# GpSimd makes the remainders of the first half of expert 2's weights

## The chip, the cores and the metric

The kernel runs on one core of a Trainium2 chip. The metric is the device time of one execution in microseconds (us). Three timed runs of the kernel before gave 667.23, 667.99 and 668.74 us, median 667.99 us. One further execution was profiled; it took 665.24 us, and its span, from the first to the last instruction, is 663.5 us.

## The reference

Three stages on 1536 tokens of 512 numbers, all in float32:

```
a   = softmax(mask(q k^T / 8 + bias)) v          # 2 x 8 heads, 768 positions, 96 local + 8 global
x   = (silu(x w_gate) * (x w_val)) w_out         # d_ff = 1536
e   = argmax(x w_router);  g = softmax(...)[e]   # 8 experts, one for each token
out[mask_e] = g * sigmoid(x w_output_gate)[e] * (relu(x[mask_e] w1[e]) w2[e])
```

`w1[e]` is 512 x 1024 and `w2[e]` is 1024 x 512. The last stage, the experts, is where the change lies.

## The kernel before

**Numbers in two parts.** TensorE multiplies in the format fp32r. So that no digits are lost, every operand is kept as a rounded part and a remainder: `whi` is the weight rounded to fp32r (ScalarE, line 637), and `wlo = raw - whi` is what rounding left (VectorE, line 640). A product is then summed from `whi*xhi`, `wlo*xhi` and `whi*xlo`.

**Weights of an expert.** They come in four transfers of 1 MB (`m2_raw`, line 643): g = 0 and 1 are the halves of `w1[e]`, g = 2 and 3 those of `w2[e]`. Each fills one `raw` buffer, and there are three of those in rotation, so the transfer after next can only be issued, on SP's queue, when both the rounding and the subtraction of an earlier buffer are done. Every buffer is made into two units of 128 x 1024 (`m2_units`), so an expert has eight units: eight roundings and eight subtractions. From unit 24 on (expert 3) a unit is cut into two pieces of 128 x 512. The first 24 units, of experts 0, 1 and 2, are whole.

**Work of an expert.** The tokens have been scattered to a table `xs` in memory by expert. For expert e, `m2_gather(e)` reads its 224 rows back (`xr`, 449.8 KB, line 957 through 538, issued by GpSimd); `m2_tokens(e)` copies each token's factor and index out of it (`fac` and `idt`, lines 963 and 964, VectorE), transposes the rows and splits them into two parts. `m2_up(e)` is the up product (line 995): its sums lie in four banks used in turn, `s0` and `s1`, then the two of `gv`; for each, ScalarE copies one half out and VectorE adds the other (`hs`, line 997), and only then may TensorE write that bank again. `m2_down(e)` is the down product (lines 1012 to 1014). Results `ot` are scattered to the output by GpSimd. Expert 0 goes another way, in two blocks of 128 tokens: `block_up` and `block_down` (lines 677 to 706), with `hh` and `hl` as the two parts of its hidden numbers and `ot` from line 705.

**What sets the order.** The code is written in the order gather of expert e+2, weights of e+1, and so on, but a scheduler of the language places each instruction in its engine's queue by its own reckoning, unless it is pinned. Every engine then works strictly in the order of its queue: an instruction that waits holds up all behind it. DMAs issued by GpSimd stand in GpSimd's queue among its arithmetic.

Of the kernel before, what the change touches and what calls it, by code (L numbers as in the profile page):

```python
# [15 lines left out]
ALU = mybir.AluOpType  # L16
# [17 lines left out]
def attn_moe_moe_kernel(  # L34
# [16 lines left out]
    nc = tc.nc  # L51
# [32 lines left out]
    def f(ap):  # L84
        return ap.bitcast(F32)
# [32 lines left out]
    def load_raw(src, dt, eng=nc.sync, after=False):  # L118
        rawn[0] += 1
        pool = rawb_p if wb_open and rawn[0] % 3 == 0 else raw_p  # L120
        raw = pool.tile([P, 2048], dt, tag="raw", name="raw")
        a = src.shape[0] // P
        ins = eng.dma_start(out=raw.rearrange("p (a c) -> p a c", a=a), in_=src.rearrange("(a p) c -> p a c", p=P))
        if after:
            tc.keep_in_program_order(ins)
        return raw
# [305 lines left out]
    def wv(ap, a):  # L432
        return ap.rearrange("p (a c) -> p a c", a=a)
# [187 lines left out]
    NWC = 4  # L621
    cnt = {"u": 0}

    def m2_unit(raw, after):
        n = cnt["u"]
        cnt["u"] += 1
        m = n
        n %= NWA + NWB + NWC
        pool = wb_p if n < NWB else wa_p if n < NWA + NWB else wc_p
        hi = pool.tile([P, 1024], F32R, tag="whi", name="whi")  # L630
        lo = pool.tile([P, 1024], F32R, tag="wlo", name="wlo")
        a = raw.shape[1]
        hv, lv = wv(hi, a), wv(lo, a)
        cuts = 1 if m < 24 else 2
        for x in range(cuts):
            o = slice(x * a // cuts, (x + 1) * a // cuts)
            ins = nc.scalar.copy(hv[:, o], raw[:, o])  # L637
            if after:
                tc.keep_in_program_order(ins)
            nc.vector.tensor_tensor(out=lv[:, o], in0=raw[:, o], in1=f(hv[:, o]), op=ALU.subtract)  # L640
        return hv, lv

    def m2_raw(e, g, **kw):
        src = w1[e][:, g * 512:(g + 1) * 512] if g < 2 else w2[e][(g - 2) * 512:(g - 1) * 512, :]
        return wv(load_raw(src, F32, **kw), 4)

    def m2_units(raw, g, after=False):
        return [m2_unit(raw[:, :, z * 256:(z + 1) * 256] if g < 2 else raw[:, 2 * z:2 * z + 2, :], after)
                for z in range(2)]

    def m2_weights(e, u=(), **kw):
        u = list(u)
        for g in range(len(u) // 2, 4):
            u += m2_units(m2_raw(e, g, **kw), g)
        return u[0:4], u[4:8]

    def scatter(src, idx):
# [162 lines left out]
    def m1_stream():  # L820
        for n in range(len(work) + 1):
            if n == len(work) - W0:
                w0.append(m2_weights(0))
# [107 lines left out]
    for _ in stream:  # L931
        pass
    u10, u20 = w0[0]
    ulast = m2_units(w0[1][0], 0, True)
    block_up(shl0, u10, hh0, hl0, scratch0, 2)
    tc.keep_in_program_order(nc.vector.tensor_copy(fac0, xr0[:, DM:DM + 1]))
# [120 lines left out]

    block_up(shl, u10, hh, hl, scratch)
    ulast += m2_units(w0[1][1], 1)
    xx1 = m2_tokens(1, nx)  # L1060
    late = [m2_raw(1, g, eng=nc.gpsimd, after=True) for g in (2, 3)]
# [6 lines left out]
    for e in range(1, NE):  # L1068
        (fac, xx), (u1, u2) = cur
        hh, hl = m2_up(e, xx, u1)  # L1070
        if e + 1 < NE:
            tk = m2_tokens(e + 1, nx)
            if e + 2 < NE:
                nx = m2_gather(e + 2)
            cur = (tk, m2_weights(e + 1))
        if e == 1:
            check_cover()
        m2_down(e, fac, hh, hl, u2)
# [306 lines left out]
```

## Time and profile before

| what | before |
|---|---|
| median of three timed runs | 667.99 us |
| the profiled execution | 665.24 us |
| its span | 663.5 us |
| TensorE busy (PE) | 632.7 us, 95% |
| VectorE busy (DVE) | 437.1 us, 66% |
| ScalarE busy (ACT) | 325.9 us, 49% |
| GpSimd busy (POOL) | 132.6 us, 20% |

Times in the rows below are microseconds from the start of the span. Expert 0's second block, and the start of expert 1, lie between 475 and 514 us; from 514 us on one expert follows another every 22 us.

### The profile page before, as it was taken

To read this page: it belongs to the slowest core of one execution; us is meant where nothing else is said; L and a number is where in the kernel's file an instruction comes from. 1 tells how busy PE (TensorE), PEld (TensorE's weight loads), DVE (VectorE), ACT (ScalarE), POOL (GpSimd) and SP (SyncE) were. 2 spreads that over 40 slices of the span, in tenths; PEclk is the share of its full clock that TensorE was granted. 3 is DMA by queue.
4 is the path that set the end of the run, shared out by engine and by line. 5 is a ranking of instruction groups with operands and counts; after the bars stand their busy time and mean duration, and the time that the engine had idled before them with its cause. 6 is when DMAs were issued, how large, how long until landed. Compare 5 with 4: busy or idle time off the path is not lost.

```text
span 663.5 us, 11770 instructions
## 1 busy us (share of the span) xinstructions
PE 632.7 (95%) x4433; PEld 547.1 (82%) x4433; DVE 437.1 (66%) x1087; ACT 325.9 (49%) x755; POOL 132.6 (20%) x180
## 2 busy tenths in 40 slices
PE   9899999999999999999999999998988999999993
PEld 8677678888888798999999999987866888888882
DVE  6899985666677998464364445555679777876330
ACT  4676866666665553131132222233467666766230
POOL 3414644444432420000000111001401100110011
PEclk9999999999999999999999999999999999999998
DMA  8779872210015545030010111122598767663000
GB/s 217 171 206 249 201 185 53 65 37 21 22 26 191 185 135 188 1 127 1 1 65 1 63 64 64 49 72 89 206 294 306 231 239 246 223 216 95 12 27 29
DMA packets 71587, 80.84 MB, mean 122 GB/s; under 512 B 43376, under 2 KB 43376, under 8 KB 71520
## 3 DMA queue, kind: packets, MB, share of 16 engines
q1 hardware_dynamic: 64960, 57.35, 30.3%
q0 software_dynamic: 6560, 22.64, 9.9%
q8 instruction: 37, 0.61, 0.4%
q14 instruction: 30, 0.25, 0.1%
HBM read 66.31 MB, written 14.26 MB: 121 GB/s over the span
## 4 chain that ended last, share of the span: by engine, by line
PE 40%; issue 34%; DVE 11%; DMA 8%; ACT 3%; POOL 2%; POOLq 0%; SPq 0%; DVEq 0%; ACTq 0%
PE ps_gv L446 6%; PE ps_gv L995 5%; DMA xs<-ypay,rw 3%; PE ps_av L396 3%; PE ps_s L995 3%; PE ps_y L995 2%; PE ps_tr L365 2%; PE ps_s L1013 2%; PE ps_s L1014 2%; PE ps_s L1012 2%; PE ps_s L334 2%; PE ps_y L1014 2%; PE ps_y L1012 2%; PE ps_y L1013 2%; DMA raw<-in_moe_w_dram 2%
## 5 line engine op out<-in xcount | busy, mean ns | idle before, releaser
L446 PE MATMUL ps_gv<-xlo,whi 128*128 128x256 f32 x576 | 164.2, 285 | 0.9 <-DVE xlo L403 0.9
L446 PE MATMUL ps_gv<-xhi,whi 128*128 128x256 f32 x576 | 164.6, 287 | 0.4 <-DVE hh L454 0.3
L446 PE MATMUL ps_gv<-xhi,wlo 128*128 128x256 f32 x576 | 164.5, 286 | 0.0
L446 PEld LDWEIGHTS ps_gv<-xlo,whi 128*128 128x128 f32 x576 | 109.8, 191 | 4.7 <-DVE xlo L403 1.3
L446 PEld LDWEIGHTS ps_gv<-xhi,whi 128*128 128x128 f32 x576 | 109.6, 191 | 4.6 <-DVE hh L454 0.5
L446 PEld LDWEIGHTS ps_gv<-xhi,wlo 128*128 128x128 f32 x576 | 110.1, 191 | 1.5 <-issue 0.3
L640 DVE TENSOR_TENSOR wlo<-raw,whi 128x512 fp32r<-128x512 f32 (+1 forms) x104 | 81.4, 810 | 18.5 <-ACT whi L637 16.5
L637 ACT CAST whi<-raw 128x512 fp32r<-128x512 f32 (+1 forms) x104 | 71.0, 721 | 34.5 <-PE ps_s L1014 11.6
L453 DVE SCALAR_TENSOR_TENSOR hh<-th,ps_gv 128x256 f32<-128x256 f32 x72 | 30.1, 418 | 74.9 <-ACT th L451 74.9
L451 ACT ACTIVATE th<-ps_gv 128x256 f32<-128x256 f32 x72 | 27.6, 384 | 88.1 <-PE ps_gv L446 87.9
L380 POOL TENSOR_TENSOR sp<-sp,rs 128x512 f32<-128x512 f32 (+1 forms) x48 | 47.8, 995 | 84.3 <-DVE rs L379 71.7
L457 ACT CAST hi<-hh 128x256 fp32r<-128x256 f32 x72 | 29.2, 405 | 56.6 <-DVE hh L454 52.7
L350 ACT ACTIVATE sp<-sp,mn 128x256 f32<-128x256 f32 (+1 forms) x96 | 46.6, 487 | 18.4 <-DVE mn L346 12.0
L611 POOL DMA_INDIRECT xs<-ypay,rw x12 | 11.9, 988 | 207.2 <-DVE rw L177 192.4
L480 PE MATMUL ps_y<-whi,lo 128*128 128x512 f32 x96 | 38.2, 405 | 1.7 <-POOL lo L458 1.6
L346 DVE CUSTOM_DVE_ANT_0 sp<-ps_s,tabs 128x256 f32<-128x256 f32 (+1 forms) x96 | 36.1, 391 | 5.3 <-PE ps_tr L365 3.6
L478 PE MATMUL ps_y<-whi,hi 128*128 128x512 f32 x96 | 38.8, 404 | 0.2
L479 PE MATMUL ps_y<-wlo,hi 128*128 128x512 f32 x96 | 38.5, 401 | 0.0
L658 POOL DMA_INDIRECT out_dram<-ot,idt x14 | 13.4, 954 | 115.9 <-ACT ot L1018 88.3
L995 PE MATMUL ps_gv<-xx,whi 128*128 128x448 f32 x112 | 36.1, 372 | 0.4 <-DVE hs L997 0.4
L396 PE MATMUL ps_av<-pT,vr 128*64 128x128 f32 x352 | 29.6, 285 | 1.5 <-DMA vr<-in_v_dram 1.2
L454 DVE SCALAR_TENSOR_TENSOR hh<-hh,ps_gv 128x256 f32<-128x256 f32 x72 | 29.9, 415 | 1.0
(265 smaller groups left out, 1398.7 us busy)
## 6 DMA issues: line engine op xcount, KB each, us to landing
raw<-in_moe_w_dram SPq DMA_DIRECT2D x30, 1024.0 KB, 5.3
xs<-ypay SPq DMA_DIRECT2D x8, 514.0 KB, 8.7
raw<-in_moe_w_out_dram POOLq DMA_DIRECT2D x4, 1024.0 KB, 5.8
xr<-xs POOLq DMA_DIRECT2D x7, 449.8 KB, 5.8
ytok<-ypay SPq DMA_DIRECT2D x12, 257.0 KB, 3.3
ypay<-in_k_dram SPq DMA_DIRECT2D x12, 256.0 KB, 4.9
qr<-in_q_dram SPq DMA_DIRECT2D x12, 256.0 KB, 4.4
vr<-in_v_dram SPq DMA_DIRECT2D x12, 256.0 KB, 4.5
```

The costliest lines, as they stand in the source:

```text
L346: nc.vector.tensor_tensor_reduce(out=sp[:, e, 0:nw], in0=pS[e][:, 0:nw], in1=tb[:, h0 + e, :], scale=-QS, scalar=3.0e38, op0=ALU.add, op1= ...
L350: nc.scalar.activation(out=sp[:, e, 0:nw], in_=sp[:, e, 0:nw], func=AF.Exp, bias=mn[:, i, h0 + e:h0 + e + 1], scale=-1.0, accum_out=sm[:, ...
L380: nc.gpsimd.tensor_tensor(out=sp[:, :, 0:nw], in0=sp[:, :, 0:nw], in1=rs.to_broadcast([P, 2, nw]), op=ALU.mult)
L396: nc.tensor.matmul(av[64 * e:64 * e + 64, j, :], vt[:, 2 * j + e, :], pT[:, e, w, :], start=(w == 0), stop=(w == len(order) - 1))
L446: nc.tensor.matmul(o, a[:, kk, fo:fo + P], x[c][:, kk, :], start=(kk == 0 and m == 0), stop=(kk == KD - 1 and m == 2))
L453: nc.vector.scalar_tensor_tensor(out=hh, in0=th, scalar=1.0, in1=pg[:, 0, :], op0=ALU.add, op1=ALU.mult)
L478: nc.tensor.matmul(o, hi[:, sl], wh, start=first, stop=False)
L479: nc.tensor.matmul(o, hi[:, sl], wl, start=False, stop=False)
L480: nc.tensor.matmul(o, lo[:, sl], wh, start=False, stop=last)
L637: ins = nc.scalar.copy(hv[:, o], raw[:, o])
L640: nc.vector.tensor_tensor(out=lv[:, o], in0=raw[:, o], in1=f(hv[:, o]), op=ALU.subtract)
L995: nc.tensor.matmul(d, a[:, kk, c], x, start=(kk == 0 and m == 0), stop=(kk == KD - 1 and m == 1))
```

## The change

The subtractions of expert 2's units of g = 0 and 1, four of 128 x 1024, are issued on GpSimd instead of VectorE. `m2_weights` loses two arguments that no call used. All other units keep VectorE.

```
-    def m2_unit(raw, after):
+    def m2_unit(raw, after, eng):
...
-            nc.vector.tensor_tensor(out=lv[:, o], in0=raw[:, o], in1=f(hv[:, o]), op=ALU.subtract)
+            eng.tensor_tensor(out=lv[:, o], in0=raw[:, o], in1=f(hv[:, o]), op=ALU.subtract)
...
-    def m2_units(raw, g, after=False):
-        return [m2_unit(raw[:, :, z * 256:(z + 1) * 256] if g < 2 else raw[:, 2 * z:2 * z + 2, :], after)
+    def m2_units(raw, g, after=False, eng=nc.vector):
+        return [m2_unit(raw[:, :, z * 256:(z + 1) * 256] if g < 2 else raw[:, 2 * z:2 * z + 2, :], after, eng)
                 for z in range(2)]
...
-    def m2_weights(e, u=(), **kw):
-        u = list(u)
-        for g in range(len(u) // 2, 4):
-            u += m2_units(m2_raw(e, g, **kw), g)
+    def m2_weights(e):
+        u = []
+        for g in range(4):
+
+            u += m2_units(m2_raw(e, g), g, eng=nc.gpsimd if e == 2 and g < 2 else nc.vector)
```

The one more line in `m2_weights` moves every later line number up by one: line 997 of before is 998 of the changed kernel. The queues of TensorE, ScalarE and SP are the same in both. VectorE's differs in one place, after expert 0's last `hl`. Of the names there, `wlo_6159`, `6163`, `6169` and `6173` are the four units that move, `wlo_6179` to `6193` expert 2's second half, `xr_6154` the gathered rows of expert 3, `hs_6035` the first sums of expert 1's up product. VectorE before:

```order
L640 TENSOR_TENSOR wlo_6159<-raw_6156,whi_6158 128x1024
L688 SCALAR_TENSOR_TENSOR hl_5865<-t_5949,hh_5864 128x256
L640 TENSOR_TENSOR wlo_6163<-raw_6156,whi_6162 128x1024
L640 TENSOR_TENSOR wlo_6169<-raw_6166,whi_6168 128x1024
L174 TENSOR_SCALAR ot_5987<-ps_y_5988,xr1_5806 128x512
L640 TENSOR_TENSOR wlo_6173<-raw_6166,whi_6172 128x1024
L640 TENSOR_TENSOR wlo_6179<-raw_6176,whi_6178 128x1024
L997 TENSOR_TENSOR hs_6035<-ps_s0_6036,hs_6035 128x224
L640 TENSOR_TENSOR wlo_6183<-raw_6176,whi_6182 128x1024
L963 COPY fac_6374<-xr_6154 112x2
L964 COPY idt_6375<-xr_6154 112x2
L640 TENSOR_TENSOR wlo_6189<-raw_6186,whi_6188 128x1024
```

VectorE in the changed kernel, the same place:

```order
L689 SCALAR_TENSOR_TENSOR hl_5865<-t_5949,hh_5864 128x256
L964 COPY fac_6374<-xr_6154 112x2
L965 COPY idt_6375<-xr_6154 112x2
L174 TENSOR_SCALAR ot_5987<-ps_y_5988,xr1_5806 128x512
L640 TENSOR_TENSOR wlo_6179<-raw_6176,whi_6178 128x1024
L640 TENSOR_TENSOR wlo_6183<-raw_6176,whi_6182 128x1024
L998 TENSOR_TENSOR hs_6035<-ps_s0_6036,hs_6035 128x224
L640 TENSOR_TENSOR wlo_6189<-raw_6186,whi_6188 128x1024
```

The four subtractions are gone; the two copies out of expert 3's rows now stand directly behind `hl`, ahead of `ot` and of the first `hs`, and wlo_6183 stands ahead of that `hs` too. GpSimd's queue before, from the scatter of expert 0's first block to the gather of expert 4's rows:

```order
L658 DMA out_0_dram<-ot0_5808,idx0_253 1536x512
L538 DMA xr_5985<-xs_243 112x1028
L538 DMA xr_6154<-xs_243 112x1028
L658 DMA out_0_dram<-ot_5987,xr1_5806 1536x512
L538 DMA xr_6393<-xs_243 112x1028
```

GpSimd's queue in the changed kernel:

```order
L659 DMA out_0_dram<-ot0_5808,idx0_253 1536x512
L538 DMA xr_5985<-xs_243 112x1028
L640 TENSOR_TENSOR wlo_6159<-raw_6156,whi_6158 128x1024
L538 DMA xr_6154<-xs_243 112x1028
L640 TENSOR_TENSOR wlo_6163<-raw_6156,whi_6162 128x1024
L640 TENSOR_TENSOR wlo_6169<-raw_6166,whi_6168 128x1024
L640 TENSOR_TENSOR wlo_6173<-raw_6166,whi_6172 128x1024
L659 DMA out_0_dram<-ot_5987,xr1_5806 1536x512
L538 DMA xr_6393<-xs_243 112x1028
```

The first subtraction stands ahead of the gather of expert 3's rows, the other three between it and the scatter of expert 0's second block.

## Rows read from the trace of the kernel before

**Rows 1.** Stages: us, busy time by engine, TensorE's clock, DMA share, GB/s.
```profile
490.00:494.00 4.00, 2.46 (x11) 1.28 (x9) 2.01 (x6) 3.32 (x6) 0.00 (x0) 1.00 1.04 277
...
502.00:506.00 4.00, 2.49 (x15) 1.84 (x13) 4.00 (x9) 3.27 (x8) 0.00 (x0) 1.00 1.05 408
...
514.00:536.00 22.00, 22.00 (x122) 18.71 (x121) 17.19 (x38) 14.55 (x32) 2.55 (x3) 1.00 0.71 239
```

**Rows 2.** TensorE's waits, 485 to 515: total us, times, longest.
```profile
PE ps_s L995 <- DVE hs L997: 1.4, 2, 1.2
PE ps_tr L1039 <- DVE xx L974: 0.9, 1, 0.9
PE ps_gv L995 <- DVE hs L997: 0.4, 1, 0.4
PE ps_y L704 <- DVE hl L688: 0.3, 1, 0.3
```

**Rows 3.** Timeline of VectorE: start, us, operation, [idle before, releaser].
```profile
493.36 1.22 DVE L640 TENSOR_TENSOR wlo<-raw,whi 128x1024 fp32r<-128x1024 f32 x1
...
497.70 0.74 DVE L174 TENSOR_SCALAR ot<-ps_y,xr 128x512 f32<-128x512 f32 x1
...
499.80 1.23 DVE L640 TENSOR_TENSOR wlo<-raw,whi 128x1024 fp32r<-128x1024 f32 x1 [0.21 <-ACT whi L637]
...
502.43 0.16 DVE L963 COPY fac<-xr 112x2 f32<-112x2 f32 x1
...
502.56 1.22 DVE L640 TENSOR_TENSOR wlo<-raw,whi 128x1024 fp32r<-128x1024 f32 x1
503.70 0.38 DVE L997 TENSOR_TENSOR hs<-ps_s,hs 128x224 f32<-128x224 f32 x1
...
506.27 1.28 DVE L640 TENSOR_TENSOR wlo<-raw,whi 128x512 fp32r<-128x512 f32 x2
```

**Rows 4.** Timeline of ScalarE: expert 2's first and fifth rounding.
```profile
490.60 1.04 ACT L637 CAST whi<-raw 128x1024 fp32r<-128x1024 f32 x1 [2.60 <-DMA raw<-in_moe_w_dram]
...
498.71 2.01 ACT L637 CAST whi<-raw 128x1024 fp32r<-128x1024 f32 x2 [1.23 <-PE ps_s L995]
```

**Rows 5.** Timeline of GpSimd: the gather of expert 3's rows.
```profile
488.24 0.55 POOL L538 DMA_DIRECT2D xr<-xs  x1 [7.08 <-PE ps_tr L971]
```

**Rows 6.** GpSimd's two-input operations, over the run: count, busy and mean, or minimum/median/maximum ns.
```profile
L380 POOL TENSOR_TENSOR sp<-sp,rs 128x512 f32<-128x512 f32 x40 | 42.7, 1069 | 73.8 <-DVE rs L379 68.4 <-ACT xhi L402 3.2 <-PE ps_tr L225 1.7
...
L380 POOL TENSOR_TENSOR sp<-sp,rs 128x256 f32<-128x256 f32 x8 | 5.0, 629 | 10.5 <-PE ps_tr L365 4.2 <-DVE rs L379 3.3 <-ACT qbuf L235 2.8
...
L458 POOL TENSOR_TENSOR lo<-hh,hi x24: 723/742/1724, 49.1 to 235.1; 128x256 fp32r<-128x256 f32 x24
```

**Rows 7.** Gathers issued at 480.56, 488.24, 509.96, 533.21: KB, us to landing.
```profile
xr<-xs POOLq DMA_DIRECT2D x1, 449.8 KB, 9.8
...
xr<-xs POOLq DMA_DIRECT2D x1, 449.8 KB, 8.0
...
xr<-xs POOLq DMA_DIRECT2D x1, 449.8 KB, 7.5
...
xr<-xs POOLq DMA_DIRECT2D x1, 449.8 KB, 5.6
```

**Rows 8.** Timeline of GpSimd and VectorE at 51 us, VectorE at 90 us.
```profile
51.15 1.04 POOL L380 TENSOR_TENSOR sp<-sp,rs 128x512 f32<-128x512 f32 x1 [1.21 <-DVE rs L379]
...
51.23 2.04 DVE L417 SCALAR_TENSOR_TENSOR raw<-raw 128x1024 int32<-128x1024 int32 x1
...
90.59 1.20 DVE L417 SCALAR_TENSOR_TENSOR raw<-raw 128x1024 int32<-128x1024 int32 x1
```

**Rows 9.** SP issues expert 3's first weights: timeline; KB, us to landing.
```profile
499.61 0.37 SPq L123 DMA_DIRECT2D raw<-in_moe_w_dram  x1
...
raw<-in_moe_w_dram SPq DMA_DIRECT2D x1, 1024.0 KB, 5.3
```

**Rows 10.** Timeline of TensorE: the third group of expert 1's up product.
```profile
504.14 0.47 PE L995 MATMUL ps_s<-xx,whi 128*128 128x448 f32 x1 [1.18 <-DVE hs L997]
```

## The prediction

> **What bounds the kernel now.** I read the table by stages first, then the list of waits of TensorE, then the three queues of VectorE, ScalarE and GpSimd around the four subtractions that move. The stages: from 514 us on TensorE is busy 22.00 of each 22 us, so nothing later can be won or lost there except by shifting the whole; between 490 and 514 it has holes, and VectorE is busy 4.00 of 4 us in each of the three stages of 4 us from 502 to 514 (one of the three alike is shown) [rows 1]. The list of waits says whose holes these are: four waits on VectorE's results, 1.4 us for `hs` into the `s` banks, 0.4 us for `hs` into `gv`, 0.9 us and 0.3 us, 3.0 us together [rows 2]. VectorE is therefore what expert 1's up product waits for, and the change takes work off exactly this engine. The reader should then ask what VectorE itself waits for there.
>
> It runs the first remainder of expert 2 at 493.36, right behind it an `hl` that TensorE waits for, the result `ot` at 497.70, and at 499.80 the first remainder of the second half (wlo_6179 in the order), which sat idle 0.21 us for ScalarE's `whi`; then the first two `hs` sums of expert 1, the second at 503.70 [rows 3]. That `whi` began at 498.71 and two of them take 2.01 us [rows 4]. So 499.8 is set by ScalarE and the weights' transfer behind it, not by VectorE's load: with the four subtractions gone VectorE would stand at the same place, waiting. From there on its list is the same as before. That is the first finding: the removed work lies in front of a wait that stays.
>
> **What the change removes.** Four subtractions of 128x1024, 1.22 us each [rows 3], 4.9 us of VectorE's time between 493.4 and 499.6. By the above it buys at most the 0.3 us that TensorE waits for `hl` [rows 2], which stood behind the first of them.
>
> **What it adds on GpSimd.** Four subtractions of 128x1024, which no row of GpSimd shows. A two-input operation of 128x512 took 1.07 us and one of 128x256 0.63 us [rows 6]: 0.44 us per 256 columns, so 1024 columns come to 1.07 + 2 x 0.44 = 1.95 us. The subtraction with the rounded output took a median of 0.74 us at 128x256 [rows 6]; at the same slope that is 0.74 + 3 x 0.44 = 2.06 us, and four times the small one would be 2.97 us. I take 2.05 us (the same operation and output, nearest row), ends 1.95 and 2.97. The Trainium skill, "GPSIMD Engine Reference" (its measured table in the section on why the gap exists), has 4497 ns for 2048 fp32 columns of this operation; half of it, 2.25 us, is an estimate from that page, and by it the sum below would be 0.2 us larger.
>
> **What it moves.** Two things, and these decide. On GpSimd the order puts the first subtraction ahead of the gather of expert 3's rows (xr_6154). Before, that gather began at 488.24 [rows 5]. Now it stands behind a subtraction that needs `whi` of 490.60 + 1.04 = 491.64 [rows 4]: it begins at 491.65 + 2.05 = 493.7, 5.5 us later. On VectorE the two small copies out of this gather (`fac`, `idt` of expert 3) are moved forward past `ot`, two remainders and the first `hs`; before they ran at 502.43, long after the landing at 488.24 + 8.0 = 496.2 [rows 3, 5, 7]. Now they are the next thing after `hl`, so VectorE reaches them at about 494.5 to 496.5 and stops until the gather has landed. Queued behind them are `ot`, the remainders of expert 2's second half and every `hs` that TensorE waits for.
>
> How long does the gather take? The four at 480, 488, 510 and 533 us landed 9.8, 8.0, 7.5 and 5.6 us after issue [rows 7]. The new one starts beside two weight transfers of 1 MB, as those at 488 and 510 did; I take 7.5 us, bounds 5.6 and 9.8. Landing: 493.7 + 7.5 = 501.2.
>
> The sum: VectorE leaves the copies at 501.2; they take 0.13 us (502.43 to 502.56) and `ot` 0.74 us [rows 3]; the next operation, wlo_6179, begins at 502.0 to 502.1 instead of 499.80, +2.2 us. A second remainder now precedes the first `hs`, so that one comes 3.3 us later; but the copies are gone from between it and the second, so the second `hs` comes 2.2 - 0.13 = 2.1 us later, and TensorE's start at 504.14 behind a wait of 1.18 us [rows 10] becomes 506.2. From there VectorE is packed to 514 and TensorE after it [rows 1]: nothing makes up the 2.1 us, and the transfers behind (each issued when a remainder frees its buffer) slip by as much. Expert 3's first weights are issued at 499.61 and take 5.3 us [rows 9]; their buffer is now freed by GpSimd's fourth subtraction, at 491.65 + 4 x 2.05 + 0.55 for the gather's issue, some 500.4 to 500.8, so they land near 506.1, just inside the shift. Cost of that: nothing, while GpSimd keeps to 2.05 us. Against the profiled run, which took 665.24 us: 667.3. The median of the timed runs is 667.99 us, 2.75 us above it; carried to that, 670.1 us.
>
> **A rule against the change.** VectorE's 128x1024 operation of line 417 took 2.04 us where it began 0.08 us after a GpSimd multiplication of 1.04 us, and 1.20 us where it began alone [rows 8]: it stood until GpSimd was done. The Trainium skill, "SBUF — State Buffer", section "Who interferes with whom", says why: a VectorE operation with two inputs in SBUF and a GpSimd operation that reads SBUF share a read port, and the later one stands for all of the earlier one. The trace agrees (0.84 us lost). Here two `hl` of VectorE, at about 492.0 and 494.5, meet GpSimd's subtractions of 491.65 and 494.25 and would end up to 1.8 us later, and TensorE with them. By the rule that is hidden where VectorE then stands for the gather anyway; where the gather is quick, it is the price that remains.
>
> **Rivals.**
> 1. The gather lands quickly (5.6 us, at 499.3). Then `ot` ends at 500.1; without the blocking wlo_6179 begins 0.35 us late and the time is 0.2 us longer; with it, wlo_6179 waits for GpSimd's last subtraction until 500.8 and the time is 0.9 us longer. 668.2 to 668.9. For it: the gather at 533 landed so. Against: it met a less busy DMA (share 0.71 there, 1.04 at 490 [rows 1]).
> 2. Faster. The postponed gather leaves the two weight transfers ahead of it alone: 449.8 KB at 277 GB/s [rows 1, 7] is 1.6 us, `whi` of 498.71 comes that much sooner, and TensorE has 3.0 us of waits on VectorE to give back [rows 2]. 666.4 us. It decides only if the gather lands within about 4 us of its issue, before 498.2 less the copies and `ot`. Against: none of the four did.
> 3. GpSimd is the bound. At 2.97 us each with the gather's 0.55 us between, the fourth subtraction ends at 504.1, expert 3's weights are issued there, land at 509.4, and their first remainder, 506.27 before [rows 3], waits until 510.0: +3.7 us, 671.7 us. For it: VectorE, where it comes first, could hold up GpSimd as GpSimd held it up in rows 8. Against: VectorE stands still for most of this time.
>
> **How the numbers follow.** The forecast (+1.1 to +3, 669.1 to 671.0) has 0.52, rival 1 0.25, rival 2 0.09, rival 3 0.14. About 0.2% (1.3 us) is what a measurement of this kernel can tell from no change. Slower by more: forecast and rival 3, 0.65 (a little of the forecast's lower end lost to "same"); within it: rival 1 and that end, 0.26; faster 0.09. The range leaves out rival 2 and the far ends (a gather of 9.8 us gives +4.4): 667.2 to 672.5.
>
> **What the profile will show.** Right: GpSimd's gather for expert 3 at 493.7; its four subtractions near 2.05 us; VectorE idle for 4 us or more before a `fac` copy, released by the DMA of `xr`; wlo_6179 near 502; TensorE's waits on `hs` grown from 1.8 us by 2 us; still no wait of TensorE after the stage. Also `hl` of line 689 lengthened to 1.7 us or more beside GpSimd. Wrong: if the `fac` copy waits under 3 us, the landing was mis-sized; if expert 3's first weights are what VectorE waits for, rival 3; if TensorE's waits shrink, rival 2.

## The result

The changed kernel is slower: 672.01 us median of 6 runs (671.83 to 673.78), against 667.61 us (665.70 to 669.62) for six runs of the kernel before taken with them. The ratio is 1.0085 [1.0062, 1.0107], or 4.1 to 7.1 us; it is an estimate of its own, and the quotient of the two medians, 1.0066 (4.4 us), lies inside its interval. Its profiled execution took 671.86 us, with a span of 669.8 us; that of before took 665.24 us, which is low for that kernel, so the two traces lie 6.3 us of span apart, more than the medians.

The same stages as in [rows 1], after the change (the stage, then busy time of PE, PEld, DVE, ACT and POOL, TensorE's clock, DMA share, GB/s):

```profile
494.00:498.00 4.00, 1.66 (x6) 1.05 (x6) 4.00 (x4) 2.86 (x5) 3.99 (x4) 1.00 0.52 167
498.00:502.00 4.00, 0.00 (x0) 0.00 (x0) 4.00 (x1) 1.43 (x2) 4.00 (x2) 0.86 0.69 260
502.00:506.00 4.00, 3.39 (x9) 2.91 (x10) 1.98 (x7) 0.00 (x0) 0.36 (x2) 0.50 0.69 208
506.00:510.00 4.00, 4.00 (x22) 3.77 (x21) 3.57 (x5) 2.61 (x5) 1.53 (x1) 0.79 0.53 140
```

From 498 to 502 TensorE does nothing at all, VectorE is "busy" with a single instruction and GpSimd with two. In the next stage TensorE has work again but a granted clock of 0.50, the lower of its two levels. TensorE's waits from 485 to 520 (engine, product, what it waited for; total us, times, longest), beside [rows 2]:

```profile
PE ps_y L705 <- DVE hl L689: 7.7, 2, 6.0
PE ps_gv L678 <- DVE t L687: 1.7, 1, 1.7
PE ps_y L703 <- ACT hh L688: 0.5, 1, 0.5
```

All of the waits on `hs` and `xx` in [rows 2] are gone; two waits for `hl`, 6.0 and 1.7 us, have come in. GpSimd's queue (start, us, operation, [idle before, releaser]), beside [rows 5]:

```profile
492.23 2.36 POOL L640 TENSOR_TENSOR wlo<-raw,whi 128x1024 fp32r<-128x1024 f32 x1 [10.13 <-ACT whi L637]
494.54 0.57 POOL L538 DMA_DIRECT2D xr<-xs  x1
495.12 7.00 POOL L640 TENSOR_TENSOR wlo<-raw,whi 128x1024 fp32r<-128x1024 f32 x3
```

And VectorE's, beside [rows 3]:

```profile
492.50 2.38 DVE L689 SCALAR_TENSOR_TENSOR hl<-t,hh 128x256 fp32r<-128x256 f32 x1 [2.94 <-ACT hh L688]
...
495.66 6.50 DVE L964 COPY fac<-xr 112x2 f32<-112x2 f32 x1
...
502.14 0.41 DVE L689 SCALAR_TENSOR_TENSOR hl<-t,hh 128x256 fp32r<-128x256 f32 x1
502.48 0.15 DVE L964 COPY fac<-xr 112x2 f32<-112x2 f32 x1
...
504.73 0.75 DVE L174 TENSOR_SCALAR ot<-ps_y,xr 128x512 f32<-128x512 f32 x1 [2.02 <-PE ps_y L705]
505.39 2.35 DVE L640 TENSOR_TENSOR wlo<-raw,whi 128x1024 fp32r<-128x1024 f32 x2
507.66 0.39 DVE L998 TENSOR_TENSOR hs<-ps_s,hs 128x224 f32<-128x224 f32 x1
```

The row to look at is the copy of 112 x 2 numbers at 495.66. It takes 0.15 us elsewhere and 6.50 us here, without any wait being shown: it has been started and stands. It ends at about 502.1, when GpSimd's run of three subtractions ends (495.66 + 6.50 = 502.16 against 495.12 + 7.00 = 502.12). It is the copy of *expert 2's* factors, whose gather was issued at 481.50 and landed 8.6 us later, at 490.1, so it does not wait for its rows. Behind it stands the last `hl` of expert 0's second block, and for that TensorE waits. The last rows show that the rest of the list then runs through, with two remainders ahead of the first `hs`, as the order had it. The `hl` at 492.50 also stood, 2.38 us for 0.42, until the first subtraction was done.

How the shift builds up along TensorE's queue (us; starts of the same instructions in the two traces):

| place | before | after | shift |
|---|---|---|---|
| matmul on the last `hl` | 494.97 | 502.61 | +7.64 |
| up product, first bank | 496.00 | 504.49 | +8.49 |
| up product, second bank | 498.52 | 508.49 | +9.97 |
| up product, fourth bank | 506.11 | 513.52 | +7.41 |
| in the down product, after the last of the old waits | 513.51 | 519.75 | +6.24 |

About 0.95 us was there before the changed place (expert 0's first `ot` at 478.73 against 477.78). The waits up to the last `hl` add 6.7, the half clock 2.3 (0.85 and 1.48: the first bank's product took 4.00 us instead of 2.52), and 3.7 us come back, as TensorE no longer waits on `hs` and `xx` (2.7 us in [rows 2], and the gaps around them).

### The profile page after: what moved, and what is told of

The parts are those of the page before. It is cut to its first block, busy times and chain, and to the rows that moved or that the text cites. A ratio compares the mean times of both kernels' runs of the same rounds, so it can differ in the third digit from the quotient of the medians.

```text
span 669.8 us, 11771 instructions
## 1 busy us (share of the span) xinstructions
PE 634.2 (95%) x4433; PEld 549.3 (82%) x4433; DVE 440.6 (66%) x1083; ACT 326.2 (49%) x755; POOL 141.7 (21%) x184
## 4 chain that ended last, share of the span: by engine, by line
PE 42%; issue 34%; DVE 8%; DMA 8%; ACT 3%; POOL 2%; SPq 1%; POOLq 0%; ACTq 0%; DVEq 0%
PE ps_gv L446 6%; PE ps_gv L996 5%; PE ps_s L996 3%; DMA xs<-ypay,rw 3%; PE ps_av L396 3%; PE ps_y L996 2%; PE ps_s L1013 2%; PE ps_s L1014 2%; PE ps_s L1015 2%; PE ps_tr L365 2%; PE ps_s L334 2%; PE ps_y L1015 2%; PE ps_y L1013 2%; PE ps_y L1014 2%; DVE wlo L429 1%
## 5 line engine op out<-in xcount | busy, mean ns | idle before, releaser
L640 DVE TENSOR_TENSOR wlo<-raw,whi 128x512 fp32r<-128x512 f32 (+1 forms) x100 | 76.5, 795 | 18.3 <-ACT whi L637 15.9
```

The source lines that it names most:

```text
L640: eng.tensor_tensor(out=lv[:, o], in0=raw[:, o], in1=f(hv[:, o]), op=ALU.subtract)
```

## The experiments

Theories at the start. **Standing**: VectorE stands for as long as GpSimd has subtractions queued. **Gather** (the forecast's): the loss hangs on the gather that is issued late. e1 to e10 compute everything; m1 to m4 leave out the kernel's whole computation and only put VectorE beside GpSimd. Each timing is against runs of the kernel before on the same chip.

**m1, the standing alone.** In each piece one VectorE operation starts 0.4 to 0.9 us into a run of subtractions on GpSimd.

```
+        for z in range(n):
...
+            pin(nc.gpsimd.tensor_tensor(out=lo[:, 0:w], in0=a[:, 0:w], in1=f(b[:, 0:w]), op=ALU.subtract))
...
+        for ins in victim(s):
+            pin(ins)
```

The `victim` is a copy of 112 x 2, an operation with two inputs in SBUF, a sum with an input from PSUM, a reduction, or a multiplication by a constant.

> A kernel of its own that leaves out the whole computation and measures GpSimd's subtractions against one VectorE operation that becomes ready about 0.5 us after the first of them begins, in 15 pieces. If GpSimd holds a port that VectorE needs, and gives it up only when it has nothing queued (theory 1): the 112x2 copy and the 128x256 operation with two SBUF inputs stand 2 us beside one subtraction of 128x1024, about 7 us beside three and 14 us beside six, and about as long beside six of 128x512 as beside three of 128x1024; with a small memset between the subtractions they stand 2 us. The sum out of PSUM and the reduction of 112x2 take 0.2 to 0.5 us whatever GpSimd does. If the port is given up after each instruction (theory 2): 2.4 us or less in every piece, three or six alike, and the 6.5 us of the changed kernel were something else.

VectorE, the copy beside one subtraction and beside three, the two-input operation beside three, the sum from PSUM, the reduction, the multiplication, the copy beside six:

```profile
5.25 1.49 DVE L46 COPY vcopy<-s 112x2 f32<-112x2 f32 x1 [0.99 <-ACT s L73]
8.87 1.45 DVE L46 COPY vcopy<-s 112x2 f32<-112x2 f32 x1 [0.99 <-ACT s L73]
...
20.32 2.23 DVE L54 SCALAR_TENSOR_TENSOR vtwo<-s,hhb 128x256 fp32r<-128x256 f32 x1 [0.47 <-ACT s L72]
28.70 0.42 DVE L59 TENSOR_TENSOR vpsum<-pm,s 128x256 f32<-128x256 f32 x1 [0.47 <-ACT s L72]
37.42 0.15 DVE L50 TENSOR_REDUCE vreduce<-s 112x2 f32<-112x2 f32 x1 [1.00 <-ACT s L73]
45.63 1.45 DVE L63 TENSOR_SCALAR vscal<-s 112x2 f32<-112x2 f32 x1 [0.99 <-ACT s L73]
...
106.40 1.45 DVE L46 COPY vcopy<-s 112x2 f32<-112x2 f32 x1 [0.99 <-ACT s L73]
```

The copy (1.49 and 1.45 us) and the two-input operation (2.23) stand, as in the kernel; so does the multiplication by a constant (1.45). The sum from PSUM (0.42) and the reduction (0.15) do not. The Trainium skill, "SBUF — State Buffer", section "Who interferes with whom", says that operations with two inputs in SBUF contend with GpSimd, that copies and multiplications can, that reductions do not, and that whoever comes first keeps the port for its whole instruction; the pieces agree. Each stood for one subtraction only, whether one, three or six were queued. "Standing" in its first form is wrong; something else in the kernel makes it last for three.

**e1, the gather of expert 3 ahead of all subtractions.**

```
+            ins = eng.tensor_tensor(out=lv[:, o], in0=raw[:, o], in1=f(hv[:, o]), op=ALU.subtract)
+            if eng is nc.gpsimd:
+                tc.add_manual_dep(ins.ins, ahead[-1].name, mybir.DependencyInfo(
+                    mybir.DependencyClass.NoSync, mybir.DependencyReason.DATA), reason="behind the gather")
...
+        ahead.append(take_rows(xr, ...).ins)
```

> The changed kernel with the gather of expert 3's rows put ahead of the four subtractions in GpSimd's queue, nothing else. By the forecast's theory (VectorE stands for a gather that comes late) the loss goes: within 0.2% of the kernel before, about 668 us. By the theory of the held port the order of the gather is no matter, and without the 0.57 us in which GpSimd issued it the subtractions follow each other more closely: 671 to 674 us, VectorE's hl or fac copy standing for 4 us or more.

667.82 us, ratio 1.0006 [0.9976, 1.0035]: the loss is gone, as "gather" expected. The trace shows another reason than that theory's. GpSimd's queue:

```profile
491.28 0.55 POOL L538 DMA_DIRECT2D xr<-xs  x1 [9.29 <-PE ps_tr L977]
491.85 4.70 POOL L642 TENSOR_TENSOR wlo<-raw,whi 128x1024 fp32r<-128x1024 f32 x2
498.66 4.79 POOL L642 TENSOR_TENSOR wlo<-raw,whi 128x1024 fp32r<-128x1024 f32 x2 [2.10 <-ACT whi L639]
```

VectorE's queue beside it:

```profile
491.56 5.29 DVE L694 SCALAR_TENSOR_TENSOR hl<-t,hh 128x256 fp32r<-128x256 f32 x1 [0.69 <-ACT hh L693]
...
499.77 1.33 DVE L969 COPY fac<-xr 112x2 f32<-112x2 f32 x1 [1.58 <-DMA xr<-xs]
```

Next to the gather's issue VectorE stood for both subtractions, 5.29 us; its `hl` had begun 0.29 us ahead of them, while the DMA was being issued. In the second pair, ahead of which GpSimd had idled, it was let go after one. The gather landed 8.5 us after its issue, and VectorE still waited 1.58 us for it, so "gather" is not what went. What fell is TensorE's wait for `hl`:

```profile
PE ps_y L710 <- DVE hl L694: 2.6, 1, 2.6
```

It was 6.0 us in the changed kernel, and the clock here is 1.00 in every stage from 490 to 510.

**e2, TensorE's clock.** The changed kernel, with 100 small matmuls ahead of the last `hl`'s.

```
+            if hold and ff == 6:
+                spin(hold, True)
...
+               xr1[:, DM + 1:DM + 2].bitcast(I32), hold=100)
```

> The changed kernel with 100 small matmuls of ones, some 5.7 us of them, put on TensorE where it waited 6.0 us for the last hl. They compute nothing that is used. If the half clock that followed that wait cost what the rows show (2.3 us: the next 19 matmuls took 5.9 us for 3.6), the time falls by about 2.3 us to 669.7 with the clock at 1.00 throughout; if the clock was no part of the loss, 672 as the changed kernel or slower by the small matmuls.

669.96 us, ratio 1.0032 [1.0003, 1.0060]. The stage after the wait, columns as above:

```profile
502.00:506.00 4.00, 3.55 (x46) 3.19 (x44) 4.00 (x7) 0.00 (x0) 2.12 (x1) 1.00 0.81 242
```

The clock is 1.00 in every stage from 494 on, and the copy still stands (6.53 us). (Its 0.68 and 0.89 in the two stages from 486 to 494 lie ahead of the changed place.) In VectorE's queue the result `ot` has slipped behind two remainders here, but TensorE waited for nothing behind the last `hl` in either trace, so the comparison holds. The median is 2.05 us below the changed kernel's; the ratio has fallen by 0.0053, 3.5 us with an uncertainty of about 2.4 from the two intervals. Both agree with the 2.3 us that the table of shifts gives for the half clock.

**e3, no copies.** `fac` and `idt` made by reductions, which m1 showed not to stand.

```
-        nc.vector.tensor_copy(fac, xr[:, :, DM:DM + 1])
+        nc.vector.tensor_reduce(out=fac, in_=xr[:, :, DM:DM + 1], axis=AX.X, op=ALU.max)
```

> The changed kernel with the small copies fac and idt of every expert made as reductions over one element, same size, same place. If only the copy is held through a run of subtractions, the operation that stood 6.5 us takes 0.2 us and the last hl comes at most one subtraction late: about 667 us, as before. If hl, with two inputs in SBUF, is held in the same way, it stands in the copy's place until the run ends: 671 to 673 us, TensorE's wait for it again near 6 us.

672.29 us, ratio 1.0073 [1.0038, 1.0107], no gain. The reductions take 0.14 us, and the next operation takes their place:

```profile
496.70 6.62 DVE L689 SCALAR_TENSOR_TENSOR hl<-t,hh 128x256 fp32r<-128x256 f32 x1
```

So it is not the copy alone: the next operation that contends, here an `hl`, stands for the run in its place.

**m2, what in the kernel makes it last.** Pieces as in m1 with three subtractions, and ahead of them a DMA issued by GpSimd, a memset, a wait for the DMA's landing, or rows as in the kernel.

```
+        if "dma" in kind:
...
+            pin(nc.gpsimd.dma_start(out=d, in_=src))
+            if "memset" in kind:
+                pin(nc.gpsimd.memset(tiny, 0.0))
+            if "land" in kind:
+                pin(nc.gpsimd.tensor_copy(tiny[0:112], d[:, 0, 0:1]))
```

> A kernel of its own that leaves out the whole computation: three subtractions of 128x1024 on GpSimd against one VectorE operation, as in the run before, which freed VectorE at the end of the first of them; 19 pieces look for what holds it through all three in the changed kernel. Theory A, a DMA that GpSimd issues right ahead of the run: only the pieces with a DMA hold VectorE about 7 us, and a memset after the DMA ends it. Theory B, the transfer in flight: the same, but the memset changes nothing, and waiting for the landing first ends it. Theory C, the waits of the subtractions on ScalarE: the pieces of kind wait hold 7 us. Theory D, operands in strided pieces: those of kind strided. Theory E, more VectorE work queued behind the one that stands: those of kind back. Where none holds, the cause is in none of these.

VectorE, first without a DMA, then twice behind one (the second time with the copy coming later), then behind a DMA for whose landing GpSimd waited before its run:

```profile
8.12 1.65 DVE L46 COPY vcopy<-s 112x2 f32<-112x2 f32 x1 [0.99 <-ACT s L81]
...
25.01 6.86 DVE L46 COPY vcopy<-s 112x2 f32<-112x2 f32 x1 [0.99 <-ACT s L81]
...
44.63 5.59 DVE L46 COPY vcopy<-s 112x2 f32<-112x2 f32 x1 [2.17 <-ACT s L81]
...
74.32 2.02 DVE L46 COPY vcopy<-s 112x2 f32<-112x2 f32 x1 [4.36 <-ACT s L81]
```

Behind the DMA the two-input operation stood even longer than the copy, 7.51 us: it began 0.29 us ahead of the run (33.76 against 34.05), while GpSimd was still issuing the DMA. That is the missing piece: a DMA issued by GpSimd directly ahead of the run makes VectorE stand for all of it. With a memset between, it still did (6.76 us), which goes against theory A's expectation that a memset ends it; a memset and the landing together are as theory B, the transfer in flight, expected them, and m4 comes back to that. The pieces with waits for ScalarE, with strided operands and with more VectorE work behind stood for one subtraction at most (1.29 to 2.35 us), which leaves theories C, D and E out.

**e4, a memset between the subtractions in the kernel.**

```
+                chain(ins.ins)
+                for _ in range(1):
+                    chain(nc.gpsimd.memset(first[:, 0:1], 0.0).ins)
```

> The changed kernel with one memset of 128x1 on GpSimd after each of the four subtractions; gather and all else in their places. If a run of subtractions holds VectorE only while they follow each other directly, fac stands 2.4 us and hl at most one subtraction more: TensorE's wait for hl falls from 6.0 to 2 to 4 us and the time to 668 to 670 us. If the memset ends nothing, fac or hl stands 6.5 us and the time is 672. By the forecast's theory of the late gather a memset changes nothing: 672.

672.94 us, ratio 1.0100 [1.0062, 1.0138]; the copy stood 6.60 us. A memset ends nothing, in the kernel as alone.

**e5 and e6, half of the change.** Only the units of g = 1, or only those of g = 0, on GpSimd.

```
-            ... eng=nc.gpsimd if e == 2 and g < 2 else nc.vector)
+            ... eng=nc.gpsimd if e == 2 and g == 1 else nc.vector)      # e6: g == 0
```

> One part of the change alone: only the units of g = 1 (the third and fourth subtraction) on GpSimd, where the gather has long been issued ahead of them and no hl of VectorE falls beside them. By the theory of the held port the loss goes with the victims: 667 to 669 us, TensorE's wait for hl under 1 us. By the forecast's theory also no loss (the gather is not late): about 667. If GpSimd's slower subtraction alone (2.36 us for 1.22) set the pace of the weights: 669 us or more with TensorE waiting for hs.

> The other part alone: only the units of g = 0, one subtraction ahead of the late gather and one behind it. By the theory of the held port two single subtractions hold VectorE 2.3 us each, hl and then fac: TensorE waits 1.7 and about 1.5 us, no half clock: 668 to 670 us. By the forecast's theory the gather is as late as in the changed kernel, so the loss stays: 670 to 672 us, fac of expert 3 waiting for its landing.

e5: 666.70 us, ratio 0.9995 [0.9972, 1.0017]. The gather was issued 4.8 us before the run, and nothing stood for longer than one subtraction (2.37 us); the remainders of the second half stood too (two in 3.92 us), and TensorE waited 2.1 us on `hs`. e6: 666.28 us, ratio 1.0010 [0.9987, 1.0033]. The gather lies between the two, so that the run behind it is one; `hl` stood 2.39, the copy 1.90 us. The 668 to 672 us expected of e6 under both theories were too high. Its gather was issued at 493.45, nearly as late as the changed kernel's 494.54, yet VectorE did not wait for it and nothing was lost; that goes against "gather". TensorE waited 2.9 us for `hl` there, in two waits. Neither version gains: what VectorE is spared, it stands.

**e7 and e8, the gather's issue on ScalarE.** e7 is the changed kernel with expert 3's gather issued by ScalarE, e8 the kernel before with the same move.

```
-        take_rows(xr, xs[e * CAP:e * CAP + USE, :]...)
+        take_rows(xr, xs[e * CAP:e * CAP + USE, :]..., nc.scalar if e == 3 else nc.gpsimd)
```

> All four subtractions stay on GpSimd; only the issue of expert 3's gather goes from GpSimd's queue to ScalarE's, at about the same time (494). The theory that a DMA issued by GpSimd directly ahead makes VectorE stand for the whole run expects the copy of expert 2's factors held by one subtraction, under 2.4 us, TensorE's longest wait for hl under 2.5 us, the granted clock of 494 to 506 above 0.9, and a time 3 to 6 us below the changed kernel's, 666 to 668.5. The rival, that it is the row of three subtractions (or the gather's traffic) whoever issues the gather, expects the copy held 6.5 us, a wait of 6 us, and 671 to 672.5.

> The kernel before with the same move of the gather's issue to ScalarE and no subtraction on GpSimd: what the move alone is worth. With the gather some 5 us later than before (about 493 against 488), expert 3's copy may wait for its landing, up to 2 us of which TensorE sees under 1: 666 to 668.5. A gain of over 1 us would mean that a gain of the run with the subtractions comes from the move.

e8: 666.58 us, ratio 0.9994 [0.9972, 1.0017], so the move itself is worth nothing. e7: 669.24 us, ratio 1.0043 [1.0023, 1.0063], better than the changed kernel but above the 666 to 668.5 expected. The long standing is gone as expected: TensorE's longest wait for `hl` is 1.7 us, and the clock 1.00 in every stage from 482 to 510. GpSimd had also idled 2.09 us ahead of its run here, so e7 by itself doesn't tell the missing DMA from the idle time; m4 does. What I had not expected came behind it. VectorE:

```profile
498.45 0.15 DVE L964 COPY fac<-xr 112x2 f32<-112x2 f32 x1
...
501.10 0.80 DVE L964 COPY fac<-xr 112x2 f32<-112x2 f32 x1 [2.10 <-DMA xr<-xs]
...
502.76 5.85 DVE L640 TENSOR_TENSOR wlo<-raw,whi 128x1024 fp32r<-128x1024 f32 x2
508.53 0.38 DVE L998 TENSOR_TENSOR hs<-ps_s,hs 128x224 f32<-128x224 f32 x1
```

Expert 3's copy now waits for the landing, as the forecast had it, and the three subtractions, which began only at 499.47 for want of `whi`, meet the remainders that VectorE makes itself: two take 5.85 us instead of 2.35, and TensorE waits 3.6 us for the `hs` behind them, after which its clock is 0.57 from 510 to 514. GpSimd was held up in its turn: its last subtraction took 3.34 us, about 1 us more than alone.

**m3, what ends it.** As m2, with other things between the DMA and the run.

```
+            elif k == "q":
+                pin(nc.sync.dma_start(out=d, in_=src))
...
+        for _ in range(pause):
+            pin(nc.vector.tensor_tensor(out=vout, in0=pm, in1=wide[:, 3, 0:256], op=ALU.add))
+        pin(nc.vector.memset(a[:, 0:1], 1.0))
```

The run waits for the column that the last line writes.

> The lock measured alone in 15 pieces (the kernel's computation is left out). Held for the whole run of three means 6.5 to 7 us for the copy 112x2, released after the first subtraction 1.4 to 2. Nothing ahead: 1.5. DMA issued by GpSimd: 6.9. The same DMA issued by SyncE: 1.5 if the issuing engine matters, 6.9 if the traffic does. DMA and then a GpSimd copy or subtraction of 256 columns that reads SBUF: 1.5 if any such instruction ends it, 6.9 if only idle time does. DMA and then 1.2, 2.5 and 4.4 us of idle time: 1.5 in all three if any idle time ends it, 6.9 in the first two if only the end of the transfer does, 6.9 in all if neither does. A DMA of 112 rows of 256 bytes: 6.9 if its size does not matter. Six subtractions behind a DMA: 14 if it lasts to the end of any run; six of half the size: 7. One subtraction, DMA, three subtractions, with the copy beside the first: 1.5. Sum from PSUM 0.4, reduction 0.15, multiply by a constant 6.9.

A miss in its main piece, and useful for it: DMA directly ahead, 1.52 us and not 6.9. In this version GpSimd waited for VectorE's column between the DMA and the run, even without a pause:

```profile
13.09 0.68 POOL L85 DMA_DIRECT2D d<-in_q_dram  x1
14.27 6.99 POOL L75 TENSOR_TENSOR lo<-a,b 128x1024 fp32r<-128x1024 f32 x3 [0.49 <-DVE a L94]
```

All pieces with such a wait (0.21 to 0.94 us) stood for one subtraction at most, the six behind a DMA too. That holds for the piece with SyncE's DMA as well, 1.11 us of waiting, so it tells nothing of issuer against traffic. Only the one piece in which GpSimd ran on without it (DMA, a subtraction of 256 columns, the run) stood for all, 6.21 us. Whether the DMA or the running on matters was then open.

**m4, DMA or running on.** As m3 without that wait.

```
+CASES = [("copy", "", {}), ("copy", "d", {}), ("copy", "t", {}), ... ("copy", "dw", ...), ... ("copy", "d", {"n": 6}), ...]
```

> The lock measured alone in 14 pieces (the kernel's computation is left out), a copy 112x2 beside a run of subtractions on GpSimd. Nothing ahead 1.5; a DMA directly ahead 6.8. A subtraction of 256 columns ahead without DMA, or three of them: 1.5 if the DMA makes the state, 6.2 if it is that GpSimd runs on from an earlier instruction. DMA and one or three one-column copies without idle time: 6.5 if only idle time ends it, 1.5 if such a copy does. DMA and three small subtractions: 6.5 if it lasts as long as GpSimd does not idle. DMA and a copy that waits for ScalarE: 1.5 to 2.4. DMA, one subtraction and then the run, with the copy beside the second: 6 if it lasts, 2.4 at most if the first subtraction ends it. A copy that comes in the second subtraction of a run without DMA: released at that one's end, under 2.4; with DMA, at the run's end, over 3.5. Subtraction, DMA, run: held to the end of the run. Six behind a DMA: 13.8. One behind a DMA: 2.2.

With nothing ahead, VectorE's copy took 1.67 us. Then: DMA; a small subtraction without DMA; DMA and a one-column copy; DMA and three; DMA and a copy that waited 0.23 us for ScalarE; no DMA, the copy coming in the second subtraction; the same behind a DMA; six subtractions behind a DMA; one:

```profile
15.13 6.86 DVE L46 COPY vcopy<-s 112x2 f32<-112x2 f32 x1 [0.99 <-ACT s L87]
24.41 2.25 DVE L46 COPY vcopy<-s 112x2 f32<-112x2 f32 x1 [0.99 <-ACT s L87]
...
44.04 6.86 DVE L46 COPY vcopy<-s 112x2 f32<-112x2 f32 x1 [0.99 <-ACT s L87]
54.05 2.02 DVE L46 COPY vcopy<-s 112x2 f32<-112x2 f32 x1 [1.74 <-ACT s L87]
...
74.92 2.08 DVE L46 COPY vcopy<-s 112x2 f32<-112x2 f32 x1 [1.39 <-ACT s L87]
...
98.84 0.54 DVE L46 COPY vcopy<-s 112x2 f32<-112x2 f32 x1 [4.36 <-ACT s L87]
107.20 3.42 DVE L46 COPY vcopy<-s 112x2 f32<-112x2 f32 x1 [4.36 <-ACT s L87]
...
124.47 13.62 DVE L46 COPY vcopy<-s 112x2 f32<-112x2 f32 x1 [1.00 <-ACT s L87]
140.50 2.18 DVE L46 COPY vcopy<-s 112x2 f32<-112x2 f32 x1 [0.99 <-ACT s L87]
```

It is the DMA: running on from another instruction is not enough (2.25 us, until the first subtraction was done), and behind a DMA it lasts through six subtractions (13.62 us). It is not the transfer: the DMA in the piece with GpSimd's wait of 0.23 us was under way until about 77.4 (issued at 73.71, 3.7 us to landing), and the copy was let go at 77.00, when the first subtraction was done (2.08 us); with six subtractions it stood long after the landing. So a quarter of a microsecond of GpSimd's waiting ends it. One small instruction does not (6.86), three one-column copies do (2.02), and so do three small subtractions (1.09). In every piece that stood to the end VectorE's copy came in the first or second instruction behind the DMA, in these two in the fourth. No piece lets it come that late in a run of long ones, so whether the number of instructions, their shortness or VectorE's late arrival decides stays open.

**e9 and e10, the same in the kernel.** A one-column copy on GpSimd between the gather and the three subtractions; in e9 it reads a unit that is not yet rounded, so that GpSimd waits, in e10 one that is.

```
+                    if x == 1:
+                        last = nc.gpsimd.tensor_copy(brake, f(late_subs[2][3][:, 0:1])).ins     # e10: late_subs[0]
+                        edge(last, ahead[-1])
...
```

> The changed kernel with one small GpSimd copy between expert 3's gather and the three subtractions, which reads a column of the third rounded unit and so lets GpSimd stand idle from about 495.1 until that unit is rounded at about 496.6. The theory that VectorE stands for the whole run only where GpSimd runs on from its DMA without idle time expects no operation of VectorE in 494 to 504 above 2.5 us, TensorE's longest wait for hl under 2.5 us, no slice of 494 to 510 with a granted clock under 0.9, and 666.5 to 669.5. The rival, that the gather ahead is enough whatever lies between, expects an operation of 5 us or more, a wait for hl above 4 us and 671 to 673.

> The same small copy at the same place, reading the first rounded unit, which is long done, so that GpSimd does not idle. If the idle time ends the state, this one stays as the changed kernel: an operation of VectorE of 6.5 us, TensorE waits about 6 us for hl, clock about 0.5 in one slice, 671 to 673. If any instruction that reads SBUF ends it, 666.5 to 669.5.

e9: 669.21 us, ratio 1.0040 [1.0024, 1.0055]; e10: 670.18 us, ratio 1.0065 [1.0046, 1.0084], a little under the 671 to 673 expected. The intervals overlap, so the times alone don't tell them apart; the traces do. GpSimd's queue in e9:

```profile
494.87 0.58 POOL L538 DMA_DIRECT2D xr<-xs  x1
496.99 0.18 POOL L669 COPY brake<-whi 128x1 f32<-128x1 f32 x1 [1.54 <-ACT whi L639]
497.14 7.08 POOL L671 TENSOR_TENSOR wlo<-raw,whi 128x1024 fp32r<-128x1024 f32 x3
```

VectorE's queue in e9:

```profile
495.98 0.15 DVE L982 COPY fac<-xr 112x2 f32<-112x2 f32 x1
...
500.19 1.74 DVE L982 COPY fac<-xr 112x2 f32<-112x2 f32 x1 [3.65 <-DMA xr<-xs]
...
502.57 3.86 DVE L645 TENSOR_TENSOR wlo<-raw,whi 128x1024 fp32r<-128x1024 f32 x2
```

GpSimd's queue in e10, where the copy does not wait:

```profile
491.57 0.20 POOL L669 COPY brake<-whi 128x1 f32<-128x1 f32 x1
491.71 6.98 POOL L671 TENSOR_TENSOR wlo<-raw,whi 128x1024 fp32r<-128x1024 f32 x3
```

VectorE's operation that it stopped in e10:

```profile
492.11 6.62 DVE L982 COPY fac<-xr 112x2 f32<-112x2 f32 x1
```

Without the wait VectorE stands 6.62 us and TensorE waits 6.1 us for `hl`, clock 0.50 in one stage; with it nothing stands longer than 2.4 us next to the run except the two remainders, 3.86 us together, the first of them 2.73 (2.5 at most was expected). In e9 the forecast's wait appears whole, 3.65 us for the gather that landed 5.3 us after its issue; TensorE then waits 3.9 us on `hs`, and the granted clock is 0.61 in 506 to 510. That last point goes against the expectation (no stage under 0.9).

No version tried beats the kernel before.

## Why the prediction was right or wrong

The direction was right. The 672.01 us lie inside the range of 667.2 to 672.5, but by luck: it reached that far for a GpSimd that bounds the kernel (rival 3), and a gather of 9.8 us would have come to about the same, and neither came. By the medians the change cost 4.4 us where 2.1 were forecast, and the mechanism that was priced is not the one that acted.

- **What the removed work was worth.** Worked out: at most 0.3 us, because a wait for ScalarE stays behind it. Too low: 3.7 us came back, the waits on `hs` and `xx` of [rows 2] and more. Whether the removed work or only TensorE's coming 7 to 10 us later took these waits away, no run separates fully. In e1, which has all four subtractions off VectorE and takes as long as before, waits on `hs` of 1.5 and 0.4 us and on `xx` of 0.9 us are there again; that speaks for the second.
- **GpSimd's subtraction.** Taken as 2.05 us, measured 2.35 to 2.41 (four, median 2.36). The slope was the multiplication's, and the 0.74 us at 256 columns with it do not give the subtraction's size: the subtraction itself took 1.23 us at 512 columns (m1, six in 7.37). The estimate of 2.25 us from the Trainium skill, "GPSIMD Engine Reference", was nearer.
- **The gather, 5.5 us later.** It was issued at 494.54 against 493.7 forecast, and the move of the copies of expert 3 was as told. But VectorE never waited for it: it reached that copy at 502.48, after the landing. The landing was mis-sized too: it was put at 7.5 us, beside two weight transfers of 1 MB, and here all 0.46 MB had moved by 498.0, 3.5 us after the issue, with a DMA share of only 0.52 from 494 to 498. The step is not wrong in itself, as the waits for it in e9 (3.65 us), e7 (2.10) and e1 (1.58) show; in the changed kernel it was hidden behind something longer. In e9, where it is VectorE's longest wait, the time is 2.7 us above its runs of before, near the 2.1 forecast. Bringing the gather forward (e1) cured the loss for another reason than the one given.
- **The step that failed** is "a rule against the change". It named the right effect, from [rows 8], and priced it at "up to 1.8 us", two `hl` standing for the rest of one subtraction each, hidden under the wait for the gather. In the trace the first `hl` did that (2.38 us). The second place was not a single subtraction but a run of three directly behind the gather's issue, and the operation was the copy of expert 2's factors, which the forecast did not count among those that contend. It stood 6.50 us with the `hl` behind it. m2 and m4 show that the DMA ahead makes the difference, e7 and e9 that without it, or with a wait of GpSimd behind it, the long standing goes. With it went about half of the loss (1.0043 and 1.0040 against 1.0085); what is left there is the wait for the gather and the remainders that stood. [rows 8] show one instruction against one and could not foretell it. Nor does the rule of the Trainium skill, "SBUF — State Buffer", section "Who interferes with whom", which also speaks of one instruction against one. Why the issue of a DMA does this, no run shows. How much it costs hangs on what TensorE has to wait: e1 lost nothing with 5.29 us of standing, as TensorE waited 2.6 us for `hl`.
- **The clock.** Put at nothing, without a reason. A wait of 6 us ended in a granted clock of 0.50 and cost 2.3 us by the table of shifts, with which e2 agrees.
- **Rivals.** 1, without the gather's wait, foresaw a standing of VectorE and priced it at 0.9 us. 2 (faster) did not come. 3 (GpSimd the bound) has nearly the measured time, 671.7 us, by another mechanism: GpSimd's run was over at 502.1, and expert 3's weights were not what anyone waited for.

The sum with the measured terms: +6.7 (waits up to the last `hl`) + 2.3 (clock) - 3.7 (old waits) = +5.3 us in the profiled pair, +4.4 by the medians.

## What to carry over

Work moved from VectorE to GpSimd runs beside VectorE only where VectorE's operations don't contend. Here 4.9 us of subtractions became 9.4 us on GpSimd, beside which two-input operations and small copies of VectorE stood (in m1 a multiplication too), and even the versions without the long standing (e5, e6, e7, e9) gained nothing. Look at the neighbours in both queues: a DMA issue of GpSimd directly ahead of a run of its arithmetic made the standing as long as the run, 6.5 us instead of at most 2.4, where VectorE's operation came early in it. And an instruction that is far too long for its size, with no wait shown, is a sign of standing; the end of another engine's run at the same time says whose.

## Not expected of the hardware

- Behind a DMA issued by GpSimd, VectorE's contending operation stood for the whole run that followed: one subtraction 2.18 us, three 6.86, six 13.62; without the DMA 1.45 to 2.35 us for runs of one, three and six. The DMA's own transfer was not the reason: in m2 the rows had landed by about 28 us, and VectorE stood until 31.87; in m4 a wait of GpSimd ended it while the transfer was under way. What in the issue does it stays open.
- A wait of GpSimd between the DMA and the run ended it wherever there was one; the shortest of them was 0.21 us. A memset (6.76 us), one small copy (6.86) or one small subtraction (6.21) did not; three small ones did (2.02 and 1.09).
- A copy of 112 x 2 numbers contends as much as one of two wide inputs; a reduction of the same 112 x 2 does not (0.15 us).
